# Long convolution with a gated MLP: one set of twiddles per frequency block, 32-bit filter transposes, and a written-out task list

## The chip, the core and the metric

The kernel runs on one core of one Trainium2 chip. The metric is device microseconds of one execution; of the kernel before, three runs are known, and their median is 205.09 us. A profile is one further look: one execution with every instruction's start and duration, in which TensorE (PE), VectorE (DVE), ScalarE (ACT), GpSimd (POOL) and the DMA queue of SyncE (SP) are separate engines that run their own instruction lists in order and wait for each other by semaphores.

## What is computed

All inputs are bf16. The reference, cut to what matters:

```python
x  = A_q                                  # [1, 2048, 512]
xn = layernorm(x)                         # no gain, no bias
# branch A: short shift of k, times v, long causal convolution per channel, skip, times xn
k_shift = sum(k_pad[:, t:t+S, :] * shift_k[:, 3-t] for t in range(4))
kv  = k_shift * v
y   = irfft(rfft(kv, 2S) * rfft(ssm_k, 2S))[:S] + kv * ssm_D
s   = xn * y
# branch B: gated MLP, 512 -> 1792 -> 512
g   = silu((gelu_tanh(xn @ w_gate) * (xn @ w_up)) @ w_down)
out = x + s * g
```

## The kernel before, in words

**Tiling.** The 2048 rows are held as 16 tiles t of 128 partitions: partition p and tile t hold row 16p+t. They are worked off in four quarters q of four tiles. For each q the MLP takes 14 feature blocks m: four matmuls for gate and four for up (128x512, all through the helper line L678), GELU on ScalarE (L1172, tile GE), the product with up on VectorE (L1175, tile HT). Then `down(q)` runs 14 matmuls for each of four row tiles. For q < 3, Silu is tanh on ScalarE (L1199) and one operation on VectorE (L1201). The last quarter uses Silu itself (L1207), a product (L1209), a sum (L1210) and its stores.

**Layernorm and its transposes.** `ln(q)` takes statistics per tile on VectorE (L861, L862, L870), the power -1/2 on POOL (L871), and writes XN (L874). For q=0 the transposed xnT is made on TensorE (L896, with the identity) in two pairs of row tiles, each pair in one PSUM bank, copied out by ScalarE and VectorE (L674, L675). For q=1 to 3 one DMA transpose on SyncE does it (L887). The first two feature blocks of q=0 are cut in two halves of 256 columns, so that they can begin with the first pair of row tiles; GELU and the product still take all 512.

**The convolution** is a discrete Fourier transform in two stages, with a complex spectrum of 32 groups of 128 rows, kept as real and imaginary rows side by side.
- Stage 1 (`stage1`) multiplies row tile t by F1[:, t], two 128x128 matrices of cosines and sines that hold the twiddle factor of t as well. It is done for the filter (16 tiles HTr, stores to the DRAM scratch ZH) and for kv (V, stores to ZK). ScalarE copies PSUM out into ASH or AST/ASX.
- Stage 2 (`tiles`, `fwd`, L1067) takes four groups at a time in 16 small 32x32 matmuls; its weights MT are the same for every group. For the filter it reads BH (from ZH) and its result goes to ZS, for kv it reads BK (from ZK).
- `spectrum(n)` multiplies the kv spectrum (KB) with the filter's (HS, loaded from ZS) on VectorE (L1134, into HB and KS), transforms back with 32 small matmuls (weights MT[1] and MT[2]), copies to BO (two buffers) and stores to ZI from ScalarE's queue.
- The last stage reads BI from ZI, multiplies by G1[:, t] (the transpose of F1[:, t], made by four DMA transposes on SyncE, L1102), and VectorE multiplies by XN and the MLP's result (L1255, L1249), adds x (L1267), and SyncE stores.

**Filter.** The filter arrives as four channel blocks Hn (128 channels x 2048 positions). `h_transpose` makes 16 transposes of 128x128 bf16 per block (L926, 64 in all), eight per PSUM bank, and two copies per block into HTr (L674 on ScalarE or L675 on VectorE); `h_fold` (L939) adds ssm_D to its first row.

**The shift.** `kshift(i)` forms kv for four row tiles with eight VectorE operations of 2048 columns (L1044 to L1052, tiles KAC, KTM, V), with the taps SKB, which POOL copies out of SKR (L1024).

**Tables.** F1 is computed on chip: 16 iotas on POOL (L731), phases on VectorE in four pieces (L761, L762, after small constants at L744 to L748), four sines of 1024 columns on ScalarE (L768). MT needs iotas and small VectorE operations (L960 to L986) and a sine with two table switches (L989, L990). GELU is another table of ScalarE, so it waits for the sines of F1 (`sin_tasks`).

**The order of the work.** Every piece above is a task with its engine, an estimated duration and its buffers. `Sched.run` is a list scheduler that plans with those estimates: among tasks that can start within SLACK of the earliest, it takes the one of lowest priority number (the constants P_...). Buffers come from pools with a fixed number of slots (four PSUM banks for gate, up and down at a time, NF_BANKS). What it finds is emitted as each engine's fixed instruction list; on the chip each engine runs its list in order. The input loads keep their own order (ORDER) at the head of SyncE's queue, except one piece of x on ScalarE's.

```python
            st, t, _, en = min(mine, key=lambda c: (c[1].prio + (self.DEFER if late.get(c[1].heavy) else 0.0), c[0], c[1].n))
```

Of the kernel before, what the change touches and what calls it, by code (L numbers as in the profile page):

```python
# [24 lines left out]
ORDER = ("w1 k0 v0 w2 k1 v1 w3 x1 d0 d1 k2 v2 k3 v3 x2 x3", "w1 k0 v0 w2 x1 k1 v1 w3 d0 d1 k2 v2 k3 v3 x2 x3",  # L25
         "w1 k0 v0 w2 k1 w3 v1 x1 d0 d1 k2 v2 x2 k3 v3 x3", "w1 k0 v0 w2 k1 v1 w3 d0 x1 d1 k2 v2 k3 v3 x2 x3")[int(0.2)]
# [8 lines left out]
P_ZS = -25.414  # L35
P_HS = 40.705
P_BK = 2.723
P_XT = 19.554
P_G1 = -59.994
P_KB = 3.323  # L40
P_PI = -12.874
P_LN1 = 8.9
P_LN2 = 29
P_LN3 = 36.208
N_HOLD = 3
P_H1 = -137.134
P_K1 = 28.68
P_KSH = 10.596
P_KV = -81.664
P_BH = 0.174  # L50
P_H2 = 37.806
P_H2E = -118.293
P_K2 = -30.393
P_MUL = -44.647
P_BO = -10.624
P_ZI = -33.146
P_Q0 = 73.801
P_DN = 67.371
P_GE = 2.281
P_HT = 1.358  # L60
P_TA = 52.481
P_TG = -66.799
P_BI = 63.435
P_Y = 45.533
P_YD = -65.898
P_GX = 54.735
P_OD = 0.974
P_HTR = 0.191
P_SKB = 74.778
P_SG = 64.83  # L70
P_SU = 50.419
# [176 lines left out]
class Pool_:  # L248
# [26 lines left out]
    def find_all(self, n):  # L275

        got = []
        while len(got) < n:
            one = self.find()
            if one is None:  # L280
                break
            got.append(one)
            self.take(one[1])
        for f, i in got:
            self.used -= 1
            for j in range(i * self.size, (i + 1) * self.size):
                self.busy[j] = False
        return got if len(got) == n else None

# [25 lines left out]
class Task:  # L315
    __slots__ = ("n", "opts", "r", "w", "emit", "prio", "deps", "lat", "nbytes", "start", "end", "eng", "nleft", "outs", "heavy")


class Sched:


    SLACK = 105.145
# [3 lines left out]
    HEDGE = 180.685  # L326
# [5 lines left out]
    QUEUE = {"ACT": 943.835, "DVE": 5.13899e+08}  # L332
    URGENT = 0.1
    DEFER = 51593
# [5 lines left out]
    def add(self, opts, emit, r=(), w=(), prio=5, lat=0.0, nbytes=0, after=(), heavy=None):  # L340
# [6 lines left out]
        t.prio = prio  # L347
# [3 lines left out]
        t.heavy = heavy  # L351
# [11 lines left out]
        t.outs = []  # L363
        t.nleft = len(t.deps)
        for d in t.deps:
            d.outs.append(t)
# [9 lines left out]
    def behind(self, t, others):  # L376

        for d in others:
            if d not in t.deps:
                t.deps.append(d)  # L380
                t.nleft += 1
                d.outs.append(t)

    def run(self):
# [3 lines left out]
        ready = [t for t in self.tasks if t.nleft == 0]  # L388
        order = []
        while ready:  # L390
            cands = []
            for t in ready:
                base = 0.0
                for d in t.deps:
                    base = max(base, d.end + d.lat + (self.SEM if not d.nbytes or t.opts[0][0] != "PE" else 400.0 if d.eng == "loads" else self.HEDGE))
                ok = True
                wants = {}
                for b in t.w:
                    if b.pool is not None and b.slot is None:
                        wants[b.pool] = wants.get(b.pool, 0) + 1  # L400
                for pool, n in wants.items():
                    av = pool.find_all(n)
                    if av is None:
                        ok = False
                        break
                    base = max(base, max(f for f, _ in av) + self.SEM)
                if not ok:
                    continue
                es = [(max(base, free.get(e, 800.0)), max(base, free.get(e, 800.0)) + dur, e) for e, dur in t.opts]
                es.sort(key=lambda x: x[1])  # L410
                cands.append((es[0][0], t, es[0][2], es[0][1]))
            assert cands, "the schedule is stuck"
            by_eng = {}
            for c in cands:
                if c[2] not in by_eng or c[0] < by_eng[c[2]]:
                    by_eng[c[2]] = c[0]
            eng = min(by_eng, key=lambda e: (by_eng[e], e))
            lo = by_eng[eng]
            mine = [c for c in cands if c[2] == eng and c[0] <= lo + self.SLACK]

            late = {}
            if eng == "PE":
                for e in ("ACT", "DVE"):
                    f = free.get(e, 800.0)
                    q = max(f - lo, 0.0) + sum(c[3] - c[0] for c in cands if c[2] == e and c[1].prio <= self.URGENT and c[0] <= max(lo, f) + self.SLACK)
                    late[e] = q > self.QUEUE[e]
            st, t, _, en = min(mine, key=lambda c: (c[1].prio + (self.DEFER if late.get(c[1].heavy) else 0.0), c[0], c[1].n))
            t.start, t.eng = st, eng
            free[eng] = en
            t.end = en  # L430
            if eng == "loads":
                t.end += self.LOAD_LAT
            elif t.nbytes:
                pipe = max(pipe, en + self.DMA_LAT / 2) + t.nbytes / (self.DMA_BW if en > loaded else self.SHARE_BW)
                t.end = pipe + self.DMA_LAT / 2
            for b in t.w:
                if b.pool is not None and b.slot is None:
                    b.slot = b.pool.find()[1]
                    b.pool.take(b.slot)
            for b in set(t.r + t.w):  # L440
                b.left -= 1
                b.last_end = max(b.last_end, t.end + t.lat)
                if b.left == 0 and b.pool is not None:
                    b.pool.release(b.slot, b.last_end)
            ready.remove(t)
            order.append(t)
            for o in t.outs:
                o.nleft -= 1
                if o.nleft == 0:
                    ready.append(o)  # L450
        assert len(order) == len(self.tasks)
# [15 lines left out]
def build_kernel(nc, A_q, A_k, A_v, A_shift_k, A_ssm_k, A_ssm_D, B_w_gate, B_w_up, B_w_down, out):  # L467
    with ExitStack() as es0:
# [21 lines left out]
        HB = at("HB", [128, 4, 2, DM], BF16, place["at"])  # L490
        F1 = new("F1", [128, NT, 2, 128], BF16)
        G1 = new("G1", [128, NT, 2, 128], BF16)
        MT = new("MT", [128, 3, 128], BF16)
        ident = new("ident", [128, 128], BF16)
        COLS = new("COLS", [128, 8], FP32)
# [3 lines left out]
        CC = new("CC", [128, 2, 128], I16)  # L499
# [21 lines left out]
        IO = at("IO", [128, 2, NT, 128], I16, kac_at)  # L521
        skr_at = kac_at + 8192
        SKR = at("SKR", [128, DM * 4], BF16, skr_at)
        C32 = at("C32", [128, 128], I32, xnT_at + 0)
        K32 = at("K32", [128, 128], I32, xnT_at + 512)
        S32 = at("S32", [128, 128], I32, xnT_at + 2368)
        Q32 = at("Q32", [128, 16], I32, xnT_at + 1024)
        PHI = at("PHI", [128, 128], I16, xnT_at + 1088)
        MSK = at("MSK", [128, 128], I16, xnT_at + 1600)
# [57 lines left out]
        R_F1 = [res(f"F1_{t}", F1[:, t, :, :]) for t in range(NT)]  # L587
        R_G1 = [res(f"G1_{t}", G1[:, t, :, :]) for t in range(NT)]
        R_M = [res("MT", MT[:])]
        R_id = res("ident", ident[:])  # L590
# [4 lines left out]
        R_CC = res("CC", CC[:])  # L595
# [15 lines left out]
        R_IO = [res(f"IO{i}", IO[:, 0, 4 * i:4 * i + 4, :]) for i in range(4)]  # L611
# [4 lines left out]
        R_S32 = res("S32", S32[:])  # L616
        R_PHI = res("PHI", PHI[:])
        R_MSK = res("MSK", MSK[:])
# [31 lines left out]
        def psl(b):  # L650
            return b.slot
# [4 lines left out]
        n_load = [0]  # L656
        last_load = [None]

        def load(name, out_ap, in_ap, w_res, w_buf, nbytes, ring="SP", r=(), rb=()):
            sem = dsem("d_" + name)  # L660
            n_load[0] += 1
            last_load[0] = S.add([("loads", 350.0)], lambda e: dma(ring, out_ap, in_ap, sem, r, w_res), r=rb, w=w_buf, prio=n_load[0], nbytes=nbytes)

        def op(engs, fn, r=(), w=(), rr=(), ww=(), prio=5, lat=0.0, after=()):
# [5 lines left out]
            return S.add(engs, emit, r=r, w=w, prio=prio, lat=lat, after=after)  # L670
# [17 lines left out]
        bF1, bG1, bMT, bid, bSKB = [B(f"F1_{i}") for i in range(4)], [B(f"G1_{i}") for i in range(4)], B("MT"), B("id"), [B(f"SKB{j}") for j in range(4)]  # L688
# [14 lines left out]
        bconst, bIO, bCC, bSKR = B("const"), [B(f"IO{i}") for i in range(4)], B("CC"), B("SKR")  # L703

        def pool_init():
            P = lambda fn, w: trk.op("POOL", fn, w=w)
            P(lambda h: h.iota(K32[:], [[1, 128]], base=0, channel_multiplier=0), [R_K32])
            P(lambda h: h.iota(Q32[:, 0:1], [[0, 1]], base=0, channel_multiplier=1), [R_Q32])
            P(lambda h: h.memset(COLS[:, 0:1], -math.pi * (1.0 - 2e-6)), [R_cols])
# [616 lines left out]
```

## Time and profile before

| | |
|---|---|
| three runs, us | 202.32, 205.09, 211.79 (median 205.09) |
| profiled execution, span from first to last instruction | 201.5 us; what lies around the span is not shown |
| busy: PE, DVE, ACT, POOL | 190.2, 153.1, 131.2, 16.5 us |
| DMA | 57.52 MB, mean 285 GB/s |
| chain that ended last | PE 69%, DMA 15%, ACT 7%, DVE 4% |

The profiled execution lies 0.8 us below the fastest of the three runs and 3.6 us below their median; nothing says which part of that lies outside the span. Matmuls are pipelined: a 128x512 matmul lasts 0.372 us on the page but the next one starts 0.216 us after it, so TensorE's progress is counted from start to start. In a timeline, brackets hold the idle time before an instruction and what ended it. In the chain of waits the columns are start, length, and what took the time. Lines of a queue (SPq) include the time in which the queue's instruction waits.

### The profile page before, as it was taken

To read this page: it belongs to the slowest core of one execution; us is meant where nothing else is said; L and a number is where in the kernel's file an instruction comes from. 1 tells how busy PE (TensorE), PEld (TensorE's weight loads), DVE (VectorE), ACT (ScalarE), POOL (GpSimd) and SP (SyncE) were. 2 spreads that over 40 slices of the span, in tenths; PEclk is the share of its full clock that TensorE was granted. 3 is DMA by queue.
4 is the path that set the end of the run, shared out by engine and by line. 5 is a ranking of instruction groups with operands and counts; after the bars stand their busy time and mean duration, and the time that the engine had idled before them with its cause. 6 is when DMAs were issued, how large, how long until landed. Compare 5 with 4: busy or idle time off the path is not lost.

```text
span 201.5 us, 3616 instructions
## 1 busy us (share of the span) xinstructions
PE 190.2 (94%) x1391; PEld 86.1 (43%) x1404; DVE 153.1 (76%) x252; ACT 131.2 (65%) x168; POOL 16.5 (8%) x40
## 2 busy tenths in 40 slices
PE   7688999999999999999998999899999999999992
PEld 2466444444444444444343343333443444444461
DVE  6999589889998989997865675664676671339994
ACT  2477766769677799979843876587888786141111
POOL 7295000030000000002100000000000000000000
PEclk9999999999999999999999999999999999999999
DMA  5999999999999778788899999989896423677934
GB/s 193 349 369 324 367 390 394 394 413 389 259 274 316 292 254 294 291 292 305 304 243 326 340 307 402 325 289 288 272 317 184 145 101 123 209 246 226 333 131 148
DMA packets 44455, 57.52 MB, mean 285 GB/s; under 512 B 12947, under 2 KB 32279, under 8 KB 43414
## 3 DMA queue, kind: packets, MB, share of 16 engines
q1 hardware_dynamic: 37638, 48.77, 74.5%
q10 hardware_dynamic: 6800, 8.52, 11.9%
q8 instruction: 11, 0.18, 0.3%
q14 instruction: 6, 0.05, 0.1%
HBM read 35.78 MB, written 18.87 MB: 271 GB/s over the span
## 4 chain that ended last, share of the span: by engine, by line
PE 69%; DMA 15%; ACT 7%; DVE 4%; issue 1%; POOL 1%; SPq 1%; ACTq 0%
PE psall L678 65%; DMA ZS<-AST 6%; DMA ZI<-BO 5%; PE psall L1067 4%; DMA BK<-ZK 3%; ACT AST L1083 2%; ACT BO L674 1%; DMA X<-in_A_q_dram 1%; DVE stats L861 1%; POOL mv L871 1%; ACT F L768 1%; ACT GE L1172 1%; DVE XN L874 1%; ACT L1172 1%; SPq L654 1%
## 5 line engine op out<-in xcount | busy, mean ns | idle before, releaser
L678 PE MATMUL psall<-xnT,Wg 128*128 128x512 bf16 (+1 forms) x232 | 55.1, 372 | 3.3 <-ACT xnT L674 1.7
L678 PE MATMUL psall<-xnT,Wu 128*128 128x512 bf16 (+1 forms) x232 | 56.1, 373 | 1.0 <-ACT BO L674 1.0
L1175 DVE TENSOR_TENSOR HT<-psall,GE 128x512 bf16<-128x512 f32 x56 | 38.1, 688 | 23.9 <-PE psall L678 15.2
L678 PE MATMUL psall<-Wd,HT 128*128 128x512 bf16 (+1 forms) x231 | 50.5, 366 | 0.3
L1172 ACT ACTIVATE GE<-psall 128x512 bf16<-128x512 f32 x56 | 33.0, 599 | 19.3 <-PE psall L678 16.1
L678 PEld LDWEIGHTS psall<-xnT,Wg 128*128 128x128 bf16 x232 | 22.1, 98 | 30.3 <-ACT xnT L674 2.3
L678 PEld LDWEIGHTS psall<-Wd,HT 128*128 128x128 bf16 x238 | 23.0, 98 | 25.4 <-issue 1.1
L678 PEld LDWEIGHTS psall<-xnT,Wu 128*128 128x128 bf16 x232 | 21.0, 98 | 28.1 <-issue 3.5
L674 ACT ACTIVATE BO<-psall 128x1024 bf16<-128x1024 f32 x16 | 16.5, 1029 | 6.1 <-DMA ZI<-BO 4.3
L1201 DVE SCALAR_TENSOR_TENSOR G<-G,psall 128x512 bf16<-128x512 bf16 x12 | 8.2, 687 | 13.8 <-ACT G L1199 13.8
L674 ACT ACTIVATE ASH<-psall 128x1024 bf16<-128x1024 f32 x16 | 16.1, 1018 | 1.5 <-PE psall L678 1.5
L674 ACT ACTIVATE KB<-psall 128x1024 bf16<-128x1024 f32 x16 | 16.0, 1026 | 1.6 <-PE psall L678 0.9
L1048 DVE TENSOR_TENSOR KTM<-KK,SKB 128x2048 bf16<-128x2048 bf16 x12 | 14.6, 1220 | 0.2
L1050 DVE TENSOR_TENSOR KAC<-KAC,KTM 128x2048 bf16<-128x2048 bf16 x12 | 14.6, 1217 | 0.1
L1134 DVE TENSOR_TENSOR HB<-KB,HS 128x1024 bf16<-128x1024 bf16 x16 | 11.0, 689 | 3.4 <-ACT KB L674 1.7
L871 POOL TENSOR_TENSOR mv<-mv,NHALF 128x4 f32<-128x4 f32 (+1 forms) x5 | 6.5, 1293 | 83.3 <-DVE mv L870 83.3
L1199 ACT ACTIVATE G<-psall 128x512 bf16<-128x512 f32 x12 | 7.1, 601 | 9.5 <-PE psall L678 9.4
L674 ACT ACTIVATE AST<-psall 128x1024 bf16<-128x1024 f32 x11 | 10.9, 1024 | 2.1 <-PE psall L678 1.8
L1207 ACT ACTIVATE G<-psall 128x512 bf16<-128x512 f32 (+1 forms) x5 | 2.6, 512 | 14.1 <-PE psall L678 14.1
L861 DVE BATCH_NORM_STATS2 stats<-X 128x6 f32<-128x512 bf16 x16 | 10.4, 673 | 0.8 <-DMA X<-in_A_q_dram 0.8
L1134 DVE TENSOR_TENSOR KS<-KB,HS 128x1024 bf16<-128x1024 bf16 x16 | 11.0, 684 | 0.0
L1083 ACT ACTIVATE AST<-psall 128x1024 bf16<-128x1024 f32 x9 | 8.9, 1022 | 2.4 <-DMA ZS<-AST 1.8
(78 smaller groups left out, 163.0 us busy)
## 6 DMA issues: line engine op xcount, KB each, us to landing
HS<-ZS SPq DMA_DIRECT2D x16, 512.0 KB, 6.1
ZH<-ASH ACTq DMA_DIRECT2D x16, 256.0 KB, 6.0
BH<-ZH SPq DMA_DIRECT2D x8, 512.0 KB, 5.2
BK<-ZK SPq DMA_DIRECT2D x8, 512.0 KB, 6.0
ZI<-BO ACTq DMA_DIRECT2D x16, 256.0 KB, 3.0
BI<-ZI SPq DMA_DIRECT2D x16, 256.0 KB, 5.0
ZK<-AST SPq DMA_DIRECT2D x11, 256.0 KB, 3.3
ZS<-AST SPq DMA_DIRECT2D x9, 256.0 KB, 5.0
```

What stands on the lines that cost most here:

```text
L674: return h.activation(o, i, ACTF.Copy)
L678: return h.matmul(o, lhsT=l, rhs=r, start=st, stop=sp)
L861: t_stats[t] = op([("DVE", 670.0)], lambda e, h, t=t: h.bn_stats(stats[:, t, :], X[:, t, :]), r=[bX[q][t % 4]], w=[bst[t]], rr=[R_X[t]], w ...
L871: t_pw = op([("POOL", 800.0)], lambda e, hd, ts=ts, n=n: hd.tensor_tensor(mv[:, ts, 3:4], mv[:, ts, 2:3], NHALF[:, 0:n, :], ALU.pow), r=[b ...
L1048: op([("DVE", dur)], lambda e, h, j=j, m=m: h.tensor_tensor(KTM[:, m.slot, :, :], kk(j), sk(j), ALU.mult), r=need + [bSKB[j], a], w=[m], r ...
L1050: op([("DVE", dur)], lambda e, h, m=m: h.tensor_tensor(KAC[:, a.slot, :, :], KAC[:, a.slot, :, :], KTM[:, m.slot, :, :], ALU.add), r=[m], ...
L1067: trk.op("PE", lambda h: h.matmul(ps(s, i)[b, :], lhsT=MT[a, k, a], rhs=data(col)[a, :], start=n < 16, stop=n >= len(todo) - 16, tile_posi ...
L1083: op([("ACT", act(1024))], lambda e, hd, p=p, a=a: hd.activation(ast["K"][a.slot].rearrange("p c d -> p (c d)"), ps(psl(p)), ACTF.Copy, sc ...
L1134: op([("DVE", dve(1024, 2))], lambda e, hd, h=h, k=k, o=o, T=T: hd.tensor_tensor(flat(T, o), flat(KB, kb[h]), flat(HS, hs, (k, 2 * h)), AL ...
L1172: op([("ACT", act(512))], lambda e, h: h.activation(GE[:, g.slot, :], bank(pg), ACTF.Gelu_apprx_tanh), r=[pg], w=[g], rr=lambda: R_bank(pg ...
L1175: op([("DVE", dve(512, 1))], lambda e, h: h.tensor_tensor(HT[:, q % 2, m, :], bank(pu), GE[:, g.slot, :], ALU.mult), r=[pu, g], w=[bHT[q][m]],
L1201: op([("DVE", dve(512, 1))], lambda e, h, g=g, pc=pc: h.scalar_tensor_tensor(out=g, in0=g, scalar=1.0, in1=pc(), op0=ALU.add, op1=ALU.mult ...
```

## The change

- **Twiddles.** F1 becomes one pair of 128x128 matrices for all t; the twiddle factor moves into the second stage, whose weights TF[:, g] now differ for each of the 32 groups. The inverse weights MI[0], MI[1] are the DMA transposes of TF and of TF2, TF turned by a quarter (real and imaginary columns exchanged, one with its sign changed), which POOL makes. G1 is one small DMA transpose. Fifteen VectorE operations and two sines (256 and 1024 columns) make all tables; every layernorm statistic waits for the last of these VectorE operations. GELU's table is loaded straight after the sines.
- **Filter.** Hn is read as 32-bit pairs: 32 transposes of 128x128 in fp32 with an fp32 identity instead of 64 in bf16; the copies out of PSUM sort the pairs into HTr, and of the eight copies three stand on VectorE and five on ScalarE (six and two before).
- **First rows.** Each row tile of q=0 is transposed into a bank of its own. Four feature blocks instead of two are cut into halves, and their GELU and product are cut too (256 columns). The weight blocks are cut 2, 4, 4, 4 instead of 4, 4, 4, 2. Loads come in another order: the first 512 KB of filter before x on SyncE, then the weights of blocks 2 to 5 before those of 0 and 1; x of q=1 earlier, the shift taps SKR later.
- **Order.** Priorities, SLACK, QUEUE and DEFER go; SEQ names every task in order ("b" picks a task's second engine), and `run` only checks buffers and assigns slots.

```diff
-        while ready:
...
-            st, t, _, en = min(mine, key=lambda c: (c[1].prio + (self.DEFER if late.get(c[1].heavy) else 0.0), c[0], c[1].n))
+        for name in SEQ.split():
+            t = self.tasks[int(name.rstrip("b"))]
+            eng, dur = t.opts[name[-1] == "b"]
...
-        F1 = new("F1", [128, NT, 2, 128], BF16)
-        G1 = new("G1", [128, NT, 2, 128], BF16)
-        MT = new("MT", [128, 3, 128], BF16)
+        F1 = new("F1", [128, 2, 128], BF16)
+        G1 = new("G1", [128, 2, 128], BF16)
+        TF = new("TF", [128, NG, 32], BF16)
+        MI = new("MI", [128, 2, 8, 128], BF16)
...
-        for i in range(4):
-            S.add([("POOL", 860.0)], lambda e, i=i: iotas(0, i), w=[bIO[i]], prio=1)
...
+        def m_phase():
+            D(lambda h: h.tensor_tensor(M16, PA[:].unsqueeze(2).broadcast_to([128, NG, 32]), KB32[:, 0:1, :].broadcast_to([128, NG, 32]), ALU.add), [R_PA, R_KB32[0]], [R_MF])
+            D(lambda h: h.tensor_scalar(M16, M16, TURN - 1, None, ALU.bitwise_and), [R_MF], [R_MF])
...
+        S.add([("DVE", 1000.0)], lambda e: f_phase(), r=[bcq], w=[bFP])
+        S.add([("ACT", 480.0)], lambda e: sin(F1, F16, R_F1), r=[bFP, bcq], w=[bF1])
+        S.add([("DVE", 1000.0)], lambda e: m_parts(), r=[bcq, bck, bFP], w=[bMP])
+        t_mq = S.add([("DVE", 1150.0)], lambda e: m_phase(), r=[bMP], w=[bMQ])
+        t_sin = S.add([("ACT", 1150.0 + 1300.0)], m_sin, r=[bMQ, bcq, bF1], w=[bMF])
+        sin_tasks = [t_sin]
...
-        FC = [(0, 4), (4, 4), (8, 4), (12, 2)]
+        FC = [(0, 2), (2, 4), (6, 4), (10, 4)]
...
-                    for j in range(8):
-                        t = 8 * hf + j
-                        o = bank16(pp[hf])[:, 128 * j:128 * (j + 1)]
-                        src = Hn[:, k, :].rearrange("p (a t) -> p t a", t=NT)[:, t, :]
-                        trk.op("PE", lambda h, o=o, src=src: h.transpose(o, src, ident[:]), r=[R_Hn[k], R_id], w=R_bank(pp[hf]), accum=True)
+                    for j in range(4):
+                        o = bank(pp[hf])[:, 128 * j:128 * (j + 1)]
+                        src = Hn[:, k, :].bitcast(FP32).rearrange("p (a t) -> p t a", t=NT // 2)[:, 4 * hf + j, :]
+                        trk.op("PE", lambda h, o=o, src=src: h.transpose(o, src, ident32[:]), r=[R_Hn[k], R_id32], w=R_bank(pp[hf]), accum=True)
...
-                    return copy(e, h, HTr[:, 8 * hf:8 * hf + 8, 128 * k:128 * (k + 1)],
-                                bank16(pp[hf]).rearrange("p (t d) -> p t d", d=128))
+                    return copy(e, h, HTr[:, 8 * hf:8 * hf + 8, 128 * k:128 * (k + 1)].rearrange("p (t c) d -> p t d c", c=2),
+                                bank16(pp[hf]).rearrange("p (t d c) -> p t d c", d=128, c=2))
...
-                trk.op("PE", lambda h: h.matmul(ps(s, i)[b, :], lhsT=MT[a, k, a], rhs=data(col)[a, :], start=n < 16, stop=n >= len(todo) - 16, tile_position=(32 * row, 32 * col)),
+                trk.op("PE", lambda h: h.matmul(ps(s, i)[b, :], lhsT=wt(col)[a, :], rhs=data(col)[a, :], start=n < 16, stop=n >= len(todo) - 16, tile_position=(32 * row, 32 * col)),
...
-            if q == 0 and m < 2:
+            if q == 0 and m < N_HALF:
...
+                    op([("ACT", act(256))], lambda e, h, p=p2[0], g=g2, c=c: h.activation(GE[:, g.slot, c], bank(p)[:, c], ACTF.Gelu_apprx_tanh), r=[p2[0]], w=[g2],
+                       rr=lambda p=p2[0]: R_bank(p), ww=lambda g=g2: [R_GE[g.slot]], after=sin_tasks)
```

## Prediction

> **What bounds the kernel now.** I read, in this order: the page's busy shares, the same shares by stage (windows cut where TensorE's idling changes), TensorE's waits, the chain of waits, and the timelines of TensorE, VectorE and SyncE's queue around the idle places.
>
> ```profile
> core 0: us, PE busy (x) PEld busy (x) DVE busy (x) ACT busy (x) POOL busy (x), PEclk, DMA share, GB/s
> 0.00:18.14 18.14, 13.22 (x118) 8.95 (x118) 15.64 (x41) 10.45 (x11) 12.15 (x37) 1.00 0.91 299
> 18.14:105.40 87.26, 86.78 (x510) 38.52 (x520) 77.17 (x120) 67.42 (x86) 4.33 (x3) 1.00 0.99 324
> 105.40:131.30 25.90, 23.95 (x224) 9.45 (x222) 15.89 (x25) 16.33 (x22) 0.00 (x0) 1.00 1.02 339
> 131.30:197.40 66.10, 65.89 (x541) 29.16 (x546) 43.05 (x62) 36.38 (x48) 0.00 (x0) 1.00 0.67 220
> 197.40:201.50 4.10, 0.33 (x4) 0.05 (x1) 1.32 (x5) 0.59 (x2) 0.00 (x0) 1.00 0.38 123
> ```
>
> Columns: window, length, then busy time of each engine. From 18.14 to 105.4 and from 131.3 to 197.4 TensorE is full, so nothing that only relieves another engine there pays. Three places are not full: the start, 105.4 to 131.3, and the 4.1 us after the last matmul. The chain through the start:
>
> ```profile
> 6.73 0.73 DVE XN L874 x2
> ...
> 11.98 0.70 DVE F L761
> 12.68 0.02 issue
> 12.70 0.44 DVE F L762
> 13.14 0.34 DVE xnT L675
> 13.48 0.02 issue
> 13.51 0.60 ACT xnT L674
> 14.11 2.08 ACT F L768 x2
> 16.18 0.02 issue
> 16.20 1.28 ACT L1172
> 17.48 0.01 issue
> 17.49 0.61 ACT GE L1172
> 18.10 0.05 issue
> 18.14 1.47 PE psall L678 x8
> ```
>
> The sine tables F (phases on VectorE L761/L762, sines on ScalarE L768) and the table switch to GELU (L1172) end at 17.49; until then no PSUM bank of gate or up comes free. What TensorE gets done meanwhile, and its later waits:
>
> ```profile
> 5.21 1.15 PE L926 MATMUL psall<-ident,Hn 128*128 128x128 bf16 x16
> 9.53 1.05 PE L678 MATMUL psall<-xnT,Wg 128*128 128x256 bf16 x8 [0.96 <-ACT xnT L674]
> 106.48 1.90 PE L678 MATMUL psall<-xnT,Wg 128*128 128x512 bf16 x8 [0.64 <-DMA xnT<-XN]
> 111.32 0.44 PE L1067 MATMUL psall<-BK,MT 32*32 32x512 bf16 x16 [0.35 <-DMA BK<-ZK]
> 128.78 1.04 PE L678 MATMUL psall<-xnT,Wu 128*128 128x512 bf16 x4 [0.78 <-ACT BO L674]
> 131.22 1.04 PE L678 MATMUL psall<-xnT,Wu 128*128 128x512 bf16 x4 [0.18 <-ACT BO L674]
> ```
>
> The idle times in brackets sum to 0.64+0.35+0.78+0.18 = 1.95; from start to start, less one 0.216 matmul each, the same places lose about 2.5. Their causes: SyncE issues the third transpose late and long ("97.32 6.93 SPq L887" in its timeline), BK's load waits behind it until 105.88, and the chain shows "118.40 9.21 DMA ZI<-BO": a store holds one of two BO buffers.
>
> **Base.** The sum is made against the profiled span, 201.5. The runs shown are 202.32, 205.09 and 211.79, so this execution stands with the fastest; I carry its difference to the median unchanged. About 2% is what a measurement of this kernel can tell from no change.
>
> **Start, until the first gate matmul.** The change computes all twiddles before the first layernorm (`after=[t_mq]`). On VectorE, from 1.20 (when the first index operation could run in before): two 128x128 integer operations at 0.34 pitch (L745), two of 256 columns at 0.36 (estimate: between L746's 0.23 for 128 and twice that), eight small ones at 0.19 (pitch of L744), and 0.72+0.45 (L761, L762 pitch): 0.7+0.7+1.5+1.2 = 4.1, so statistics begin at 5.3 instead of 3.64. X rows queue on SyncE behind 512 KB of filter, but in before such a piece had landed by 5.0 and 384 KB more at the 300 to 370 GB/s of the stage takes about 1.2; so X and VectorE are ready together. The first gate and up weights end 2.0 MB into the loads, near 8.5 at that rate, before 10.2. Statistics to XN took 3.09 in before (3.64 to 6.73, through the 1.07 POOL power); XN begins near 8.3 and ends at 9.0. XN to the first gate matmul took 2.07 (7.46 to 9.53), where a pair of rows was transposed and evicted as one; in after each row has its bank, so at least 1.0 (transposes 0.25 with 0.22 drain, one 0.6 eviction). I take 1.2: first gate matmul at 10.2 (bounds 10.0 to 11.1), 0.7 later than 9.53.
>
> **Start, what comes after it.** The sines, one of 256 and one of 1024 columns (1.15), and the GELU table (1.28) end on ScalarE near 8.1, before its first eviction; so from 10.2 GELU runs at once. To stand where before stood at 18.14, TensorE needs 24 of 256 columns at 0.11 (half of 0.216) = 2.6, eight XN transposes at 0.062 = 0.5, and 24 of the 32 new filter transposes (eight run in the idle time before). A bf16 transpose takes 0.062 from start to start; the 32-bit one moves as many columns of twice the bytes, and is not in the trace: not below 0.062, not above 0.216, a matmul of four times the columns. Same column count is the nearer row: 0.065, so 1.6. That gives 10.2+2.6+0.5+1.6 = 14.9, a gain of 3.2.
>
> Off it go waits of TensorE between 13 and 17: VectorE evicts three filter tiles (HTr, two of them ahead of the HT multiplies) and eight half-wide HT, ScalarE five. HTr copies took 0.61 each on VectorE; the new ones write every other row, so 0.61 to 1.22 (L1255, the longest 1024-column PSUM operation); I take 1.1. Two delay the second HT from about 13.7 to 15.9, and up-matmuls have four banks, 1.8 of work, to fill: about 1.0 idle. Net gain of the start 2.2.
>
> **Middle.** By 512-column matmuls at 0.216 and tile groups at 0.36 and 0.58, q=2's gate work begins 98.0 into after's TensorE list and 100.0 into before's; the difference is mostly the later start of counting. In SyncE's order the q=2 transpose now stands ahead of two ZS stores and of the last BH load; VectorE's list gives its XN at about 92.5, landing took 9.1 at the median, so 101.6 against about 103 needed: the 0.8 lost at 105.5 goes. BK's load follows a 6.93 issue and one store, and lands in 5.3: about 105.6; but its tiles come 12 matmuls after q=2's first instead of 20, at 105.5: 0.1 to 0.8 of wait, I take 0.3 for the 0.5 lost. The first two inverse groups are 9.9 of TensorE work apart instead of 7.0, so the 9.2 ZI store is over before its buffer is wanted: 1.2 goes. Four F-to-G1 transposes on SyncE (7.44) become two of the same size and a quarter-size one (about 4.2); the second waits for the first to land, but it stands behind a BH load that waits longer. That load needs all of ZH, and nine of the sixteen ZH stores move behind later evictions on ScalarE, the last to about 56: 6.0 to land, 5.2 for BH, 67.5 against first BH tiles due near 75; cover 7. Gain 2.5-0.3 = 2.2.
>
> **What is hidden.** VectorE loses 4.4 (F phases), 1.9 (MT), about 3.1 (C, Q, ident, three HTr, constants) and gains 4.0: -5.4. ScalarE loses 4.4 of sines, 0.45 and two 1.28 tables of MT, gains 1.6 and 2.9 (three HTr): about -3. POOL loses 16 iotas (3.4) and gains two identities and two TF2 turns (like SKB, 0.69 each and up), which stand ahead of q=2's power; POOL is idle from 18 on but for 4.3. All at nothing: 18.14 to 105.4 has no VectorE-made TensorE idling to remove. Were that cover gone, a microsecond of VectorE is one of TensorE. The tail keeps its 4.1: last Silu, two VectorE operations and the store are the same. Tile groups keep their counts; MI or TF replace MT as weights, at nothing.
>
> Sum: -2.2-2.2 = -4.4: 201.5 to 197.1, and 205.09 to 200.7.
>
> **Rivals.** (a) 32-bit transposes at 0.216: 24 x 0.15 = 3.6 back: 204.3. For it: twice the bytes; against it: columns set every other matmul's pitch.
>
> (b) TensorE runs slow again. Its first eight warm-up matmuls start 0.427 apart, later ones 0.216, and the gaps of 1.06 and 1.34 before 7.20 and 9.53 cost no speed. From the last warm-up matmul (about 5.1) to the hold matmuls near 9.3 after has 4.2 with 16 transposes only; before has 2.5 (5.2 to 7.75). If that cools it, 3.4 us go at 0.427 for 0.216: 1.7 lost, 202.4. The Trainium skill, "TensorE: Matmul & The Clock Gate", Parts 1 and 4, says that an idle window of some 3.4 us halves the clock and that transposes do not count as busy in the same way; by that rule this rival comes true when a window falls into the gap, and the trace, whose gaps are shorter, neither bears it out nor contradicts it.
>
> (c) Only the start pays; each middle wait is replaced by another, as BK's closer tiles suggest: 205.09-2.2 = 202.9.
>
> (d) Slower: VectorE is late for V. Its list has the fourth V product end near 84.4, and TensorE asks at 84.7; cover 0.3. SKR now lands after about 1.9 MB more, near 20.4 for 15.3, SKB near 24, KAC due at 27.3. If loads or HTr copies make VectorE slip, every microsecond over 0.3 goes to TensorE, and XN of q=2 behind it. It outweighs the gain of 4.4 from a slip of 4.7; a slip of 6 gives 206.4, one of 9 gives 209.4, the 2% line. Against: before's VectorE had idle 0.3 to 0.9 per HT there, and 5.4 less work.
>
> **Chances.** Forecast 0.60, by itself 197 to 203 (first gate matmul 10.0 to 11.1, BK wait 0 to 0.8, 0 to 2 us of bank waits, and a spread between runs that in before is mostly upward); 0.42 of it below 201.0, the 2% line, 0.18 above. (a) 0.08, (b) 0.10 and (c) 0.08 are within 2%. (d) 0.14, since a slipped VectorE also drags loads behind it: 0.04 within 2%, 0.10 beyond. So faster 0.42, within 0.48, slower 0.10. The range, 197 to 206.5, reaches over (a), (b), (c) and the lower half of (d) and leaves out the rest of it and some of the forecast's edges.
>
> **What would show it.** Right: first gate matmul near 10.2 with no GELU wait behind it; transposes of Hn 0.062 to 0.08 apart; no ACT BO wait near 116 to 131; windows full from about 17. Wrong: Hn transposes 0.2 apart (a); 256-column gate matmuls 0.2 apart at 10 to 13 (b); waits on xnT or BK longer than 0.8 (c); V matmuls waiting for DVE V at 85 to 90 (d).

## The result, and the profile after

| | before | after |
|---|---|---|
| median, us (4 runs each) | 204.12 | 224.28 (222.28 to 226.31) |
| ratio | | 1.099, interval 1.090 to 1.108 |
| profiled span, us | 201.5 | 223.2 |

The kernel became 10% slower; 200.7 and the range 197 to 206.5 missed it. Later ratios leave disturbed executions out, so they can differ a little from the ratio of two medians. The copies into HTr, first before (min/median/max in ns, then when the first and the last began), then the groups of the page after (count, then busy time and mean ns of one, then idle time before them):

```profile
L675 DVE COPY HTr<-psall x6: 672/673/673, 14.7 to 17.6; 128x1024 bf16<-128x1024 bf16 x6
L674 ACT ACTIVATE HTr<-psall x2: 1017/1024/1030, 9.4 to 10.3; 128x1024 bf16<-128x1024 bf16 x2
```

```profile
L593 ACT ACTIVATE HTr<-psall 128x1024 bf16<-128x1024 bf16 x5 | 23.3, 4762 | 4.8 <-DVE HTr L594 4.3
...
L594 DVE COPY HTr<-psall 128x1024 bf16<-128x1024 bf16 x3 | 13.9, 4758 | 0.4 <-PE psall L834 0.4
```

Eight copies of 1024 columns, 4.7 to 5.0 us each on both engines, 37.2 of busy time in all. In before they took 0.67 (VectorE) and 1.02 (ScalarE). They are now the chain through the start:

```profile
9.69 1.15 PE psall L597 x7
10.87 0.38 ACT GE L1032
11.25 4.59 ACT HTr L593
...
16.98 4.70 DVE HTr L594
21.71 4.70 ACT HTr L593
...
34.85 9.21 ACT HTr L593 x2
```

TensorE's timeline shows who pays: the first gate matmul stands where it was forecast, at 10.22, and GELU follows at once; then PSUM banks come free only as the copies end. The first stage-1 matmul of the filter, at 19.67 in before (first line), stands at 39.58 (last line).

```profile
19.67 0.38 PE L678 MATMUL psall<-HTr,F 128*128 128x512 bf16 x1
```

```profile
10.22 1.92 PE L597 MATMUL psall<-xnT,Wg 128*128 128x256 bf16 x16
...
15.89 0.61 PE L597 MATMUL psall<-xnT,Wu 128*128 128x256 bf16 x4 [2.87 <-ACT HTr L593]
...
17.49 3.31 PE L597 MATMUL psall<-xnT,Wu 128*128 128x256 bf16 x16
21.73 0.61 PE L597 MATMUL psall<-xnT,Wg 128*128 128x256 bf16 x4 [0.93 <-DVE HTr L594]
26.45 2.74 PE L597 MATMUL psall<-xnT,Wg 128*128 128x256 bf16 x12 [4.11 <-ACT HTr L593]
...
39.58 1.03 PE L597 MATMUL psall<-HTr,F 128*128 128x512 bf16 x2 [5.29 <-ACT HTr L593]
```

Two losses are visible. The brackets, with 1.78 more before 44.11, sum to 15.0. And sixteen 256-column matmuls take 3.31 where the same group takes 1.92 at 10.22: the granted clock fell (0.69 in the window 15 to 20, 0.50 in 25 to 30). It did so behind these waits; with quick copies and without the waits it stays at 1.00 (e1, below). The middle did not get rid of its waits either; BK and the BO buffers still hold TensorE:

```profile
133.13 0.44 PE L929 MATMUL psall<-BK,TF 32*32 32x512 bf16 x16 [1.02 <-DMA BK<-ZK]
...
149.52 1.04 PE L597 MATMUL psall<-xnT,Wg 128*128 128x512 bf16 x4 [0.58 <-ACT BO L593]
...
151.95 0.44 PE L929 MATMUL psall<-BK,TF 32*32 32x512 bf16 x16 [0.53 <-ACT BO L593]
```

**A ledger.** For each profiled execution I take the start of the last matmul, the TensorE gaps after 45 us (each start-to-start gap over 0.5, less 0.216), and what lies behind the last matmul. What is left of the difference to before is put down to the start. The last column is no finer than about 0.4: e3 and e9 reach their first stage-1 matmul at 22.38 and 22.36 and still differ by 0.4 there, because shorter gaps later on are in it too.

| kernel | last matmul | gaps after 45 | behind it | start against before |
|---|---|---|---|---|
| before | 197.46 | 2.61 | 4.04 | |
| after | 219.70 | 4.46 | 3.50 | 22.24 - 1.85 = +20.4 |
| e1_rows | 200.04 | 7.38 | 3.46 | 2.58 - 4.77 = -2.2 |
| e3_bf16_filter | 196.78 | 3.56 | 3.52 | -0.68 - 0.95 = -1.6 |
| e6_before_rows | 200.73 | 3.76 | 4.07 | 3.27 - 1.15 = +2.1 |
| e7_third_bo | 196.70 | 1.80 | 3.50 | -0.76 + 0.81 = +0.05 |
| e9_warm | 195.49 | 2.65 | 3.51 | -1.97 - 0.04 = -2.0 |
| e10_warm_rows | 195.40 | 2.87 | 3.50 | -2.06 - 0.26 = -2.3 |

So after lost about 22.6 in the start against its own list with quick copies (e1), 15.0 of it in waits for HTr. The other 7.6 are, by estimate, mostly matmuls at half clock: the granted clock was 0.50 from 16.9 to 20.3, from 23.8 to 30.6 and from 37.4 to 47.7, TensorE was busy for 13.8 of these 20.5 us, and half of that is 6.9.

### The profile page after: what moved, and what is told of

It is laid out like the page before. It is cut to its first block, busy times and chain, and to the rows that moved or that the text cites. A ratio compares the mean times of both kernels' runs of the same rounds, so it can differ in the third digit from the quotient of the medians.

```text
span 223.2 us, 3556 instructions
## 1 busy us (share of the span) xinstructions
PE 198.4 (89%) x1388; PEld 90.3 (40%) x1388; DVE 160.0 (72%) x240; ACT 146.8 (66%) x170; POOL 11.7 (5%) x25
## 4 chain that ended last, share of the span: by engine, by line
PE 65%; ACT 14%; DMA 10%; DVE 6%; ACTq 2%; issue 2%; POOL 0%; POOLq 0%
PE psall L597 60%; ACT HTr L593 10%; DMA ZI<-BO 7%; PE psall L929 4%; DMA BK<-ZK 3%; ACTq L575 2%; DVE HTr L594 2%; ACT GE L1041 1%; ACT AST L593 1%; DVE TF L685 1%; DVE stats L775 1%; ACT BO L593 0%; ACT ASH L593 0%; PE psall L834 0%; ACT ASX L945 0%
## 5 line engine op out<-in xcount | busy, mean ns | idle before, releaser
L597 PE MATMUL psall<-xnT,Wu 128*128 128x512 bf16 (+1 forms) x240 | 58.9, 384 | 3.3 <-ACT HTr L593 2.9
L1044 DVE TENSOR_TENSOR HT<-psall,GE 128x512 bf16<-128x512 f32 x52 | 35.0, 687 | 25.6 <-PE psall L597 16.4
L597 PE MATMUL psall<-Wd,HT 128*128 128x512 bf16 (+1 forms) x238 | 52.4, 367 | 0.3 <-ACT GE L1041 0.3
L597 PEld LDWEIGHTS psall<-xnT,Wg 128*128 128x128 bf16 x240 | 23.2, 100 | 33.1 <-ACT HTr L593 4.4
L1041 ACT ACTIVATE GE<-psall 128x512 bf16<-128x512 f32 x52 | 30.3, 608 | 9.3 <-PE psall L597 8.9
L597 PEld LDWEIGHTS psall<-xnT,Wu 128*128 128x128 bf16 x240 | 23.6, 103 | 31.3 <-issue 4.3
L593 ACT ACTIVATE HTr<-psall 128x1024 bf16<-128x1024 bf16 x5 | 23.3, 4762 | 4.8 <-DVE HTr L594 4.3
L593 ACT ACTIVATE ASH<-psall 128x1024 bf16<-128x1024 f32 x16 | 16.0, 1024 | 7.3 <-PE psall L597 5.2
L593 ACT ACTIVATE KB<-psall 128x1024 bf16<-128x1024 f32 x16 | 15.6, 1024 | 4.5 <-PE psall L929 3.1
L597 PE MATMUL psall<-HTr,F 128*128 128x512 bf16 x32 | 10.3, 425 | 7.1 <-ACT HTr L593 7.1
L594 DVE COPY HTr<-psall 128x1024 bf16<-128x1024 bf16 x3 | 13.9, 4758 | 0.4 <-PE psall L834 0.4
L945 ACT ACTIVATE AST<-psall 128x1024 bf16<-128x1024 f32 x10 | 10.0, 1023 | 2.8 <-DMA ZS<-AST 1.9
```

The costliest lines, as they stand in the source:

```text
L593: return h.activation(o, i, ACTF.Copy)
L594: return h.tensor_copy(o, i)
L597: return h.matmul(o, lhsT=l, rhs=r, start=st, stop=sp)
L945: op([("ACT", act(1024))], lambda e, hd, p=p, a=a: hd.activation(ast["K"][a.slot].rearrange("p c d -> p (c d)"), ps(psl(p)), ACTF.Copy, sc ...
L1041: op([("ACT", act(512))], lambda e, h: h.activation(GE[:, g.slot, :], bank(pg), ACTF.Gelu_apprx_tanh), r=[pg], w=[g], rr=lambda: R_bank(pg ...
L1044: op([("DVE", dve(512, 1))], lambda e, h: h.tensor_tensor(HT[:, q % 2, m, :], bank(pu), GE[:, g.slot, :], ALU.mult), r=[pu, g], w=[bHT[q][m]],
```

## The experiments

The theory after the result: the order in which a copy writes HTr is the whole loss, and the start gains what was forecast once it is mended. The rival: the 32-bit transposes, or the new order around them, cost something themselves.

### Only the order of the writes (e1_rows)

```diff
-  HTr[...].rearrange("p (t c) d -> p t d c", c=2)   <-  PSUM "p (t d c) -> p t d c"
+  HTr[...].rearrange("p (t c) d -> p t c d", c=2)   <-  PSUM "p (t d c) -> p t c d"
```

> The changed kernel with only the loop order of the eight filter copies turned: row by row (t, c, d), so that what is written runs along a row, instead of (t, d, c), where each two bytes written jump by 1 KB to the other row and back. Theory W (the write order costs, and the late filter is the whole loss): the copies fall from 4.7 us to 1.0 to 1.2 on both engines, TensorE's first stage-1 matmul comes near 23 instead of 39.6, its half-speed stretch after 39.6 goes, and the time is 200 to 206. Rival T (the filter as 32-bit pairs is slow to copy whatever the order, since both halves of a word are read apart): copies stay above 4, time stays 220 to 226. Rival L (the written-out list loses time elsewhere too): copies fall, but the time stays above 208.

Measured: 203.88 against 204.7 for before, ratio 0.992 (0.986 to 0.998). The loop order alone is worth the 20 us: what was lost comes back, and the whole change is then at most 1.4% faster than before. The same values go to the same places, row after row now (min/median/max in ns):

```profile
L593 ACT ACTIVATE HTr<-psall x5: 1017/1024/1024, 11.1 to 21.1; 128x1024 bf16<-128x1024 bf16 x5
L594 DVE COPY HTr<-psall x3: 1216/1225/1225, 13.9 to 19.6; 128x1024 bf16<-128x1024 bf16 x3
```

ScalarE does not notice that PSUM is now read at every other element; VectorE takes 1.22 for 0.69. TensorE is full from 9.5 to 51.6 and its clock stays at 1.00.

### Five orders at once (e2_orders)

```diff
+  o = {(0,0): "t c d", (0,1): "d t c", (1,0): "t c d", (1,1): "d t c", (2,0): "d c t", (2,1): "t d c", (3,0): "d c t", (3,1): "c d t"}[k, hf]
+  HTr[...].rearrange("p (t c) d -> p " + o, c=2)    # PSUM likewise
```

> The changed kernel with the eight copies in five loop orders, all giving the same HTr: (t,c,d) along the row; (t,d,c) as changed, one; (c,d,t), (d,t,c) and (d,c,t), which jump at every element too but come back to the same row after 4 or 8 writes instead of 2. Theory W1 (a jump at every element costs): all but (t,c,d) take 4 to 5 us. Theory W2 (coming back at once to the row just written costs): (t,d,c) 4.7, (c,d,t) about half, the ones with 8 rows 1.0 to 2. Theory T (reading halves): (d,t,c) and (t,d,c), which read both halves one after the other, differ from (c,d,t) and (t,c,d).

Measured (221.67 in all): on ScalarE "d c t" 4.71 and 4.76, "t d c" 4.69, "d t c" 5.02, "t c d" 1.02; on VectorE "d t c" 4.71, "c d t" 4.75, "t c d" 1.43. It makes no difference whether the writes go round two, four or eight rows: whatever leaves the row at every 2-byte element takes about 4.6 ns an element.

### 64 bf16 transposes again, everything else as changed (e3_bf16_filter)

```diff
-  for j in range(4): h.transpose(bank(pp[hf])[...], Hn[...].bitcast(FP32)..., ident32[:])
+  for j in range(8): h.transpose(bank16(pp[hf])[...], Hn[...], ident[:])
   HTr copies: "p (t d) -> p t d", row after row
```

> The changed kernel with the filter part undone: 64 bf16 transposes and contiguous copies as in the kernel before, the list, twiddles and halves kept, as are the engines of the copies. Theory W: copies 0.6 on VectorE and 1.0 on ScalarE, time as with the row order or up to 1 us below it, 200 to 206. Rival L: above 208.

Measured: 201.75, ratio 0.987 (0.979 to 0.994). Without the filter part the change is a small gain, 0.6 to 2.1%. Beside e1, the 32-bit transposes themselves save a little of TensorE: they start 0.111 apart at full clock against 0.062, 32 of them for 64, and the first stage-1 matmul starts at 22.05 with them and at 22.38 here. The time does not show it: e1's median is 2.1 above e3's.

### The filter part alone, in the kernel before (e4_before_pairs, e6_before_rows)

e4 adds to before the 32-bit transposes, the fp32 identity and the copies as changed ("t d c"); e6 the same with rows ("t c d").

> The kernel before with the filter part alone added: 32 transposes of 32-bit pairs, an fp32 identity, copies in the order (t,d,c). Theory W: eight copies of 4.7 us, six of them in a row on VectorE and two on ScalarE, hold up stage 1 by about 20 us and the time is 215 to 230. Rival T predicts the same. Rival L (the list is at fault): under 210.

> The kernel before with the 32-bit filter part alone, but with copies that write row after row. If the order of the writes was the whole loss of that part (229.4 with pairs), this stands at the time of before, 203 to 206: 32 transposes at 0.111 for 64 at 0.062 save 0.4 of TensorE in a stage that waits for GELU anyway, and six VectorE copies at 1.22 for 0.67 add 3.3 there. Rival: VectorE's 3.3 delay the sine phases or the first products, 206 to 208. If fp32 transposes themselves were the trouble: above 215.

Measured: e4 229.44, ratio 1.124 (1.118 to 1.130), copies 4.7 to 5.0. So the part is as dear without the rest of the change, and dearer, as six of the eight copies stand one behind the other on VectorE. e6 207.78, ratio 1.024 (1.019 to 1.029): its rival came true. Six copies at 1.21 for 0.67 are 3.2 us more of VectorE just where TensorE waits for it:

```profile
21.74 0.60 PE L679 MATMUL psall<-HTr,F 128*128 128x512 bf16 x2 [1.96 <-DVE HTr L676]
```

In the changed kernel three such copies stand on VectorE, with room. That a 32-bit filter which is written well pays at all is not shown: with bf16 transposes in its place e1's 203.88 becomes e3's 201.75, and e10's 201.39 becomes e9's 200.42, and the intervals of the ratios overlap both times.

### What makes a write dear (e5_runs, e12_strides)

Both use the kernel of e3, where PSUM holds whole rows, so that every variant writes the same values. e5 writes b adjacent elements of a row and then goes on to the next of eight rows; e12 stays in the row and writes single elements, s apart, in s passes.

```diff
 e5:  "p t (a b) -> p a t b"     # runs of b, then another row
 e12: "p t (a b) -> p t b a"     # single elements, b apart, same row
```

> The changed kernel with bf16 filter transposes, so PSUM holds whole rows, and every copy into HTr writes runs of b elements of one row before it goes on to the next of eight rows, values unchanged. On ScalarE in the order of its queue b = 2, 4, 8, 16, 1; on VectorE b = 2, 4, 8. Theory A, each jump to another row costs about 4.6 ns: b=1 4.7 us, b=2 2.4, b=4 1.2, b=8 and 16 the floors of 1.02 (ScalarE) and 0.7 (VectorE). Theory B, only a 2-byte element without its neighbour is dear (half a word): b=1 4.7, everything from b=2 on at 0.7 to 1.25. Theory C, any write that is not in whole rows is dear: 4.7 for all of them.

> The changed kernel with bf16 filter transposes; each copy into HTr stays in its row, but writes it in several passes of single 2-byte elements, s elements apart. On ScalarE in the order of its queue s = 2, 4, 8, 32, 64 (4 to 128 bytes), on VectorE s = 8, 2, 32. Theory A, a 2-byte element whose neighbour does not follow at once costs 4.6 ns wherever the next one lies: 4.7 us for all eight. Theory B, what is dear is only leaving the neighbourhood of the last write (16 to 64 bytes): about 1.0 to 1.3 at s = 2 and 4, and 4.7 from s = 8 or 32 on.

| what is written next | ScalarE, us | VectorE, us |
|---|---|---|
| another row after 1 element | 4.71 | |
| another row after 2 | 1.04 | 1.07 |
| another row after 4 | 1.02 | 0.67 |
| another row after 8 | 1.02 | 0.69 |
| another row after 16 | 1.02 | |
| same row, 4 bytes on | 1.31 | 1.50 |
| same row, 8 bytes on | 2.45 | |
| same row, 16 bytes on | 4.87 | 4.71 |
| same row, 64 bytes on | 4.68 | 4.75 |
| same row, 128 bytes on | 5.13 | |

The pairs of e5 on ScalarE, then e12 on ScalarE at 16 bytes and on VectorE at 4:

```profile
12.04 1.04 ACT L593 ACTIVATE HTr<-psall 128x1024 bf16<-128x1024 bf16 x1
```

```profile
26.37 4.87 ACT L593 ACTIVATE HTr<-psall 128x1024 bf16<-128x1024 bf16 x1 [0.44 <-PE psall L835]
```

```profile
19.86 1.50 DVE L594 COPY HTr<-psall 128x1024 bf16<-128x1024 bf16 x1
```

The first theory of e5 (4.6 ns for each jump) fell: pairs that jump at every second element would have taken 2.4 and take 1.04. Theory B, a lone half word, held there. In e12 its theory A fell; B held with an edge at 16 bytes, but 8 bytes cost 2.45 where it had about 1.3. A count fits it: 1024 elements at 4, 8 and 16 bytes visit 256, 512 and 1024 pieces of 16 bytes, and 1.31, 2.45 and 4.87 on ScalarE are 5.1, 4.8 and 4.8 ns a piece. Together: these copies behave as if a 2-byte write without its neighbour cost about 4.7 ns for every new piece of 16 bytes, and two neighbours written together did not. One thing stays open. In e5 and e12 the PSUM side is read in the same order as HTr is written, so they step both sides at once. That the write alone can cost it is shown by after, which reads PSUM in order and takes 4.69, and that a read of every other element is free on ScalarE by e1; that the 8 and 16 bytes of e12 belong to the write and not to the read is argued, and no run separates them. The Trainium skill, "SBUF — State Buffer", in its note under "Door 1: The DMA port swizzle", gives lines of 16 bytes and says that each crossing to a new line costs unless a line is hit at least twice. If the cost of e12 lies in its writes, the 16 bytes agree with these runs, but "twice" does not: two hits 8 bytes apart in a line still took 2.45, and only two adjacent ones 1.04. Why an unpaired 2-byte write is dear is not shown by any run.

### The middle: a third BO buffer, an earlier transpose (e7_third_bo, e8_early_xnt)

```diff
 e7: BO = new("BO", [128, 3, 2, DM], BF16); pBO = Pool_("BO", 3)      # and its semaphore
 e8: the last five loads (X, KK, V, X, V) emitted after the transpose xnT<-XN of the second quarter
```

> The changed kernel with bf16 transposes and plain copies (201.75 in the run before), and three BO buffers instead of two. If the ZI stores hold TensorE in the middle, its waits for BO (1.1 us in that profile, 2.4 in the one with row order) go and the median falls by about 1, to 200.8. Rival: the stores are as slow as before and the next thing that needs them or the queue waits instead (BK, xnT of the third quarter), no change: 201.3 to 202.2.

> The same kernel (201.75), with the second quarter's DMA transpose ahead of the last five loads on SyncE's queue (X twice, V twice, KK once, 2.5 MB). If it is late because it shares the DMA engines with loads issued just ahead of it, it lands near 45 to 48 instead of 52.7, TensorE's wait for it at 52.8 (0.5 to 1.2) goes, and the median falls by 0.5 to 1: 200.8 to 201.3. Rival: the last KK and V pieces come 5 us later, VectorE's shift slips behind them, and the kernel stays or gets slower: 201.7 to 204.

Both are e3 with one thing added. e7: 202.2 with a ratio of 0.994 (0.990 to 0.998), not below e3's 201.75 and 0.987 of the earlier series, though the gaps after 45 fell from 3.56 to 1.80 and no wait for BO is left. In the profiled execution the start gave the 1.7 back (ledger): TensorE ran at a granted clock of 0.50 from 9.6 to 13.0.

```profile
9.53 1.43 PE L597 MATMUL psall<-AST 128*128 128x512 bf16 x3
10.75 3.00 PE L597 MATMUL psall<-xnT,Wg 128*128 128x256 bf16 x16
```

e8: 203.14, ratio 0.996 (0.992 to 1.001). The wait for xnT at 52.8 is gone, and 0.86 and 0.80 for GELU and 2.01 for BO stand further on. Both times lie where the rivals had them, e7's for another reason. Neither move was a gain by itself.

### Keeping the clock up (e9_warm, e10_warm_rows, e11_warm_early)

```diff
+  for _ in range(4 if j == 0 else 0):      # before the first transposes of XN, into their own bank
+      mm(h, bank(pp[0]), ZERO[:, 0:128], ZERO, True, True)
```

e9 is e7 with these four matmuls; e10 is e9 with the 32-bit filter in rows; e11 is e9 with e8's move.

> The kernel with bf16 transposes, plain copies and three BO buffers (202.2 in the run before, half of its executions at a mean clock of 0.99), with four 512-column matmuls of zeros between the first filter transposes and those of XN, about 1.0 us in a gap of 2.1. If the clock drops because nothing but transposes runs for more than 3.4 us there (in that profile the clock rose at 6.1 and matmuls went to 0.427 from 9.5 to 13), executions at 0.99 vanish and the median falls by 0.5 to 0.9, to 201.4. Rival: the drop has another cause (power of the loads' stage, the machine), the share of executions at 0.99 stays and the time stays at 201.9 to 202.5.

> The same kernel with 32-bit filter transposes and copies row after row. If fp32 transposes gain what their pitch says (32 at 0.111 for 64 at 0.062, 0.4), and VectorE's three copies at 1.22 for 0.69 cost nothing, it is 0.3 to 0.5 below the one with bf16 transposes. Rival: the longer VectorE copies (1.6 in all) or the fp32 reads delay the products behind them, and it is level or 0.5 to 1 above.

> The kernel with bf16 transposes, three BO buffers and the four matmuls, and the second quarter's DMA transpose ahead of the last five loads. With two BO buffers that move took the wait for xnT away and waits for BO (2.0) and GELU (1.7) stood in its place. If BO was the bound behind it, it is now 0.3 to 0.8 below the kernel without the move. Rival: the GELU waits at 59 and 130 come from the move itself and stay: level or up to 1 above.

Measured: e9 200.42, ratio 0.985 (0.979 to 0.992), the lowest median of all. TensorE's timeline:

```profile
6.96 1.03 PE L597 MATMUL psall<-AST 128*128 128x512 bf16 x4
...
10.22 1.92 PE L597 MATMUL psall<-xnT,Wg 128*128 128x256 bf16 x16
```

The expectation had 201.4 for it. In the profiled executions of e9, e10 and e11 the clock stays at 1.00 through the start. Without the four matmuls but with the same list ahead of the gap, it falls to 0.50 for 3.4 us in three of five: in e7 and e5 at 9.6 and 9.7, in e12 at 9.1, not in e3 and e8. For executions without a profile only the mean clock is on record, not where it was lost; one such drop of 3.4 us makes a mean of 0.991 to 0.992. Of e3, e7 and e8 12 of 28 had 0.992 or less, of e9 and e11 none of 12, of e10 two of six (0.983, over 206 us), of before 3 of 47. But e7 and e8 ran on another chip than e9 to e11; on the latter's chip it was 1 of 4 for e3 and 4 of 10 for e1. So that the four matmuls keep the clock up is likely and not settled, and that this made e9 faster is not shown: e3's ratio of 0.987 is level with e9's, and within e7 the six executions at 0.997 and above have a median of 201.85, the six below 202.36, half a microsecond apart where the trace of one lost 1.6.

e10: 201.39, 0.990 (0.983 to 0.997), no gain over e9, so its rival came true; its first stage-1 matmul is 0.3 earlier than e9's, and a 1.75 wait for xnT at 53.8 takes more than that back. e11: 200.56, 0.987 (0.982 to 0.992), level with e9, as its rival said: the move stayed without effect also with a third buffer, and the 0.92 wait for GELU near 59.7 comes with it.

## Why the prediction was wrong, point by point

- **The step that failed** is the price of the copies: "HTr copies took 0.61 each on VectorE; the new ones write every other row, so 0.61 to 1.22 (...); I take 1.1". They took 4.7, on ScalarE too, where I had charged nothing for the order. The path was in the prediction: late copies, late PSUM banks, idle TensorE. It stood there with 1.0 of idling between 13 and 17; after has 15.0 of such waits between 13 and 44, and matmuls at half clock behind them, which were not in the sum. The upper end came from the longest 1024-column row of the page, L1255, which writes along its rows, as the HTr copies of before do. So the feature in question, where consecutive writes land, was in neither end, and neither bounded it from above. e1 and e2 isolate it: the same copy in rows brings 224.3 to 203.9.
- **Rival (d)** named "loads or HTr copies make VectorE slip" at 84 us, with slips of 5 to 9. Copies were the cause; but the time went at 10 to 45 through PSUM banks, not at V, and the size (over 20) was beyond its 9.
- **Start:** the first gate matmul at 10.2 (10.22), GELU at once, and a net gain of 2.2 were right for the list itself: e1 shows -2.2. The match is in part luck. Two errors of the gain cancel: 24 transposes at 0.111 instead of 0.065 cost 1.1 more, and the 1.0 of bank waits did not come. So do two on the way to 10.2: in after the statistics begin at 5.96 instead of 5.3, because the phase operation L685 took 1.23 and not 0.72, and they reach XN 2.5 later, not 3.09.
- **Middle:** "Gain 2.5-0.3 = 2.2" did not come. With quick copies the gaps were 3.6 (e3) to 7.4 (e1) against 2.6 in before. The two-buffer wait stayed (1.1 in e3, 1.8 in e1 for BO), the one in front of the third quarter shrank from 0.64 to 0.44 in e3 and was 0.75 in e1, BK's was 0.7 to 1.6 instead of 0.3, and a wait that I had not looked for appeared: the second quarter's transpose, issued at 34.05 in e3 just behind 2.5 MB of loads, took 14.7 to issue and lands at 52.7; TensorE, now earlier, asks at 52.3. That is rival (c), the start alone paying: it had 202.9 for 205.09, a ratio of 0.989, and e1 has 0.992, e3 0.987. In after the wait does not show, as TensorE is late. The transpose on SyncE's queue and TensorE's wait for it, in e3:

```profile
34.05 14.70 SPq L800 DMA_TRANSPOSE xnT<-XN  x1
```

```profile
52.80 2.75 PE L597 MATMUL psall<-xnT,Wg 128*128 128x512 bf16 x12 [0.47 <-DMA xnT<-XN]
```

- **Rival (a):** half true. The 32-bit transpose starts 0.111 after the last one, inside the bounds 0.062 to 0.216 and off the value taken.
- **Rival (b)** happened, in other executions than the profile of after: e7 shows it at its place and price (1.6 between 9.5 and 13, priced 1.7). In after the clock fell too, but later and behind the waits for HTr. The Trainium skill's rule, "TensorE: Matmul & The Clock Gate", Part 1, of a free-running window of some 3.4 us, agrees with the trace: in e7 the clock rises at 6.2 and falls at 9.6, with only transposes between; in e3 it rises at 6.8 and does not fall. In e9, with matmuls in the gap, it rises at 6.1 and does not fall.
- **Hidden work** stayed hidden: with quick copies no wait for VectorE's V products is left in the middle, and no wait for POOL appeared. The tail, kept at 4.1, became 3.5; no run shows why.

## What to carry to other kernels

Before a copy is costed by its columns, look at where consecutive elements of its output land: a 2-byte output whose innermost step is not 1 cannot be priced by a row of the trace that writes along its rows (4.69 against 0.67 to 1.22 here), and swapping two loops in the access pattern mends it without changing a value. When the row for a price does not share the feature in question, the upper end is open, and the range has to say so. A gain ahead of transfers that share a queue is only worth what the transfers leave: the waits taken away in the middle here were answered by others, so that no run gained by it. A gap of some 4 us that holds only transposes can cost the clock; four matmuls put into it delayed nothing here, as the first gate matmul stayed at 10.22.

## What the runs showed of the hardware

- Copies from PSUM into SBUF that write single 2-byte elements, each to another row, took 4.69 us for 1024 on ScalarE and on VectorE alike, about 4.6 ns an element, even with PSUM read in order (after). Pairs of neighbours that go to another row after every second element took 1.04 and 1.07 (e5). Single elements 4, 8 and 16 bytes apart took 1.31, 2.45 and 4.87 on ScalarE, with PSUM read at the same step (e12).
- Reading PSUM at every other 2-byte element is free on ScalarE (1.02 in e1 and in e3) and takes VectorE from 0.69 to 1.22.
- A 128x128 fp32 transpose starts 0.111 after the one before, a bf16 one 0.062, at full clock; at a granted clock of 0.50 the fp32 one starts 0.213 after (in after, from 16.9 on).
- A stretch of about 3.4 us with nothing but transposes can halve TensorE's granted clock for as long again: it did in the profiled executions of e5, e7 and e12, and not in those of e3 and e8, which have the same list there.
